# Linear attention and two MLPs on one core: k and v of a head pair loaded in two requests of 64 partitions each

## The chip, the cores and the metric

The kernel runs on one core of a Trainium2 chip. The metric is the device time of one execution in microseconds (us). TensorE (PE) multiplies matrices, VectorE (DVE), ScalarE (ACT) and GpSimd (POOL) work element by element, SyncE (SP) issues DMA requests.

## The reference

```python
kv  = einsum('bhsd,bhse->bhde', k, v)        # batch 4, heads 8, seq 576, head_dim 64
out = einsum('bhsd,bhde->bhse', q, kv)
x   = out / sqrt(mean(out*out, -1) + 1e-6) * g_norm    # then (2304, 512)
h   = x @ w_in;   x = softplus(h) @ w_out    # first MLP, 512 -> 2048 -> 512
h   = x @ w_in2;  y = leaky_relu(h, 0.01) @ w_out2     # second MLP
```

All in float32; the output is (2304, 512).

## The kernel before

The attention works in 16 units; a unit is a pair of heads of one batch entry, four units a batch entry, u even and odd alternate. 576 rows of a head don't divide into 128 partitions: 512 rows stand as 4 rows on each of 128 partitions, and 64 "left rows" remain.

`load(u)` issues the loads on SP: q, k and v of the unit, each one request [128, 2 heads, 4 rows, 64] with pieces of 1024 bytes, into rings `lda` of five buffers. At the first unit of a batch entry it also loads the left rows of all eight heads, into `ldr`: k and v as [64 partitions, 8, 64] in pieces of 256 bytes, q as two requests of 64 partitions. For b = 0 these four are issued on ACT, else on SP. The lower half of `ldr` for k and v is zeroed by POOL at the start.

`T(u)` copies q and k so that a row of two heads is contiguous (`qp`, `kp`; `copy_to`, lines 406 to 410, on ACT, DVE or POOL), transposes q on PE (line 479), forms k-transposed times v for both heads in four products (`f_kv`, line 487) and a fifth one of the left rows (`f_kvl`, line 492), masks it to two blocks (`kvm`, line 505) and copies the transposed q out of PSUM (`qt`, line 422 on DVE, 420 on ACT). At even units a transpose takes the left rows of q of this unit and the next one (line 483), copied to `qtl`. `O(u)` multiplies (line 527; left rows of two units, line 534), `normal` does the norm (`xn`), `X` transposes back (line 612, and 623 for left rows) into `xy`, by an eviction on ACT (line 600) or DVE (line 602). A float32 product appears in the trace as two records of PE, a transpose as one.

The MLPs follow: their weights are loaded and unpacked by `decode_w` (line 647 and 652 issue the loads) beside the attention; the first products of the MLP are those of line 984, six records each, among the last of the attention; most of the run is lines 894, 1151 and 1156.

The order is written by a planner at build time: each `op()` states engines and costs, and `Plan.run` places the operations on engines. Its first 500 placements are a list written out by hand, `FIRST`: a letter for the engine (E is PE, A, D, P, S, and G for requests that ACT issues) and the number of the `op()` call, counted from 0. Each engine executes its operations in that order, so one that waits holds up what stands behind it. After the list the planner chooses by its own costs.

Of the kernel before, what the change touches and what calls it, by code (L numbers as in the profile page):

```python
# [21 lines left out]
class Plan:  # L22
# [10 lines left out]
    DMA_BY = {"S": "S", "G": "A"}  # L33

    FIRST = """
    S7 E26 S0 S80 G6 S9 G5 S8 S1 G4 P40 S2 G3 D27 S85 E44 E42 S10 E32 S13 A82 S14 S15 A83 S11 A81 E29
    S24 D41 S12 D30 E45 S23 D28 D84 S38 S16 A90 E33 A31 S37 S19 E34 E46 D35 S39 D47 A36 D91 E69 A43 S17
    D87 E52 A88 S20 D48 D55 A86 E68 S18 A53 D89 P100 S22 A72 D54 A70 E102 S21 P101 E104 A92 D73 E57 D71
    S50 E60 E105 A58 S49 D103 A74 P56 D59 S51 A75 E106 D76 E61 S66 A107 D25 D78 S65 A108 E62 D79 E134
    S67 D77 A63 S110 D93 A64 E132 S109 A136 P166 E135 E116 A167 D94 P119 D95 A138 E168 D139 A117 D137  # L40
    E170 E171 A133 D118 P120 A169 E124 D96 A140 E172 E178 D97 A141 A173 E125 D142 A174 D145 A98 D144
    E126 E180 S131 E121 D127 E200 A179 D143 S129 P185 S113 A128 D186 A122 E198 D99 A123 S115 E182 A202
    P213 A199 S114 D181 E187 D203 A183 E201 S146 P212 E190 A204 E191 S111 D184 A321 S130 D205 D188 E192
    A206 S112 P236 E214 D189 E228 A207 D208 E216 P235 S175 A229 E217 S151 D211 D209 A215 A193 S176 E218
    E230 P262 D219 S177 E248 A194 D210 A231 E232 A324 S195 D220 S196 D322 E251 S197 E250 A254 A249 D325
    S222 E266 S245 A252 E264 E274 S225 D265 A233 E237 D255 D253 A147 E240 S227 E481 P263 A238 D234 S226
    A148 D149 E241 S221 A256 D150 P281 A257 S223 A275 E242 D258 S246 E267 A156 D261 S224 A243 D259 A239
    E268 A244 E276 S247 D260 A152 E283 E278 S273 D269 D277 A270 S333 D154 E297 D153 S271 E294 P308 A300
    D155 A279 S272 E286 E296 P309 S338 D282 A158 D280 S291 E287 A295 D157 D159 A298 E288 E484 S293 A284
    D299 A289 S292 A290 D160 E317 D301 E482 D161 A302 D162 A303 A318 P356 D304 E312 A285 E313 D163 P357  # L50
    D307 A164 D305 E310 E314 D306 P380 E319 A311 E353 A320 D315 P381 D165 A316 E369 A354 E368 A372 D355
    A330 E358 D373 E361 A370 E362 A359 D371 E363 E366 P396 A374 D364 A360 D365 A375 E382 A327 P397 D376
    E384 E385 A367 D379 D377 A383 E391 D378 E386 A334 E389 A392 D387 P420 E393 D328 A388 A390 E408 D336
    A394 D335 P421 D395 E409 S343 A410 E401 E402 D337 A412 A339 D413 E403 D411 A340 E398 E406 D341 A414
    D404 E485 A415 S348 A407 D416 S323 A399 D419 E429 A405 D342 A400 E431 A430 E424 D417 E422 E425 A423
    D418 A346 D345 E426 A344 E436 D432 D427 E433 D347 A428 S581 A437 S332 E439 D351 A349 E438 D350 S326
    A442 D331 A483 E450 N461 A440 E488 D352 A486 A434 D443 D441 E491 A477 D435 A451 D478 E489 A444 A445
    A463 D446 E492 A479 D449 D447 A460 E452 D490 E454 D448 E500 A453 A455 D493 D480 A487 E458 E456 D464
    N462 E503 A494 D465 A495 E504 D468 A466 D496 E501 A507 D469 E546 D467 A470 D472 E550 D510 A502 A473
    """.split()  # L60

    def __init__(self):
# [105 lines left out]
def linear_attention_two_mlps(  # L168
# [32 lines left out]
    nc = tc.nc  # L201
    B, H, S, D = q.shape
# [35 lines left out]
    def ring(pool, name, n, shape, dt=F32):  # L238
        return [pool.tile(shape, dt, name=f"{name}{i}") for i in range(n)]
# [190 lines left out]
    def load(u):  # L430
        b, hp = unit(u)
        hs = slice(2 * hp, 2 * hp + 2)
        for nm, src in (("q", q), ("k", k), ("v", v)):
            def fn(e, nm=nm, src=src):
                nc.sync.dma_start(
                    out=lda[nm][u % NLD],
                    in_=src[b, hs, 0:4 * P, :].rearrange("h (p r) d -> p h r d", r=4),
                )

            op({"S": 0.73}, fn, (), [(nm, u % NLD)])  # L440
        if u % NPAIR:
            return
        e_ = "G" if b == 0 else "S"
        for nm, src in (("k", k), ("v", v)):
            def fn(e, nm=nm, src=src):
                (nc.scalar if e == "G" else nc.sync).dma_start(
                    out=ldr[nm][b % 2][:RL], in_=src[b, :, 4 * P:S, :].rearrange("h p d -> p h d")
                )

            op({e_: 0.58}, fn, (), [(nm + "r", b % 2)])  # L450
        for x in range(2):
            def fn(e, x=x):
                (nc.scalar if e == "G" else nc.sync).dma_start(
                    out=ldr["q"][b % 2][x * RL:(x + 1) * RL],
                    in_=q[b, NPAIR * x:NPAIR * (x + 1), 4 * P:S, :].rearrange("h p d -> p h d"),
                )

            op({e_: 0.29}, fn, (), [("qr", b % 2, x)])

    def T(u):  # L460
# [29 lines left out]

        def f_kvl(e):
            nc.tensor.matmul(kv, kl[:, h2, :], vl[:, h2, :], start=False, stop=True)  # L492

        for j in range(2):
            n = 2 * P
            op(
                {"PE": 0.22 if i or j else 0.33}, lambda e, j=j: f_t(e, j),
                [("qp", i)] + ([] if i or j else [("qr", b % 2, x) for x in range(2)]), [("ps", p0 + j)],
            )
            if j:  # L500
                op({"PE": 0.88}, f_kv, [("kp", i), ("v", u % NLD)], [("ps", p1)])
                op({"PE": 0.22}, f_kvl, [("kr", b % 2), ("vr", b % 2)], [("ps", p1)])
# [11 lines left out]
            if i == j == 0:  # L514
# [883 lines left out]
```

## Time and profile before

| | us |
|---|---|
| runs shown: median (lowest to highest of 3) | 781.49 (781.37 to 782.99) |
| profiled execution, device time | 784.06 |
| span of the profiled execution | 782.1 |
| busy time of PE in it | 767.8 |

The span runs from the first to the last instruction; times of rows count from its start. A row of the timeline gives start, duration and, in brackets, the idle time before it with what ended it. Line numbers are those of the kernel before.

### The profile page before, as it was taken

How to read it: one execution, taken by the hardware profiler on the slowest of the kernel's cores; microseconds unless marked ns; L12 is line 12 of the kernel's file. 1: busy time of each engine (PE TensorE's matmuls, PEld its weight loads, DVE VectorE, ACT ScalarE, POOL GpSimd, SP SyncE). 2: the span in 40 equal slices, each digit the busy share in tenths (PEclk: the TensorE clock that was granted, in tenths of full speed). 3: DMA queues.
4: the chain of work that ended last, by engine and by line, in shares of the span. 5: the costliest groups of instructions: out<-in, count | busy, mean ns of one | idle time of the engine just before them, and what ended most of it. 6: DMA issues, size and time to landing. Idle time of an engine off the chain costs nothing.

```text
span 782.1 us, 13225 instructions
## 1 busy us (share of the span) xinstructions
PE 767.8 (98%) x5029; PEld 763.6 (98%) x5029; DVE 679.3 (87%) x1084; ACT 544.2 (70%) x930; POOL 20.9 (3%) x37
## 2 busy tenths in 40 slices
PE   6899999999999999999999999999999999999997
PEld 6899999999999999999999999999999999999997
DVE  3999999999899897996899999998899877886666
ACT  4789999788676775764588788885677645554441
POOL 2330000000000000000000000000000000000000
PEclk8999999999999999999999999999999999999999
DMA  9995768685784794683678969785875772562814
GB/s 284 289 312 166 288 225 308 248 295 200 307 321 166 266 340 150 264 304 106 255 279 293 332 213 414 306 301 193 315 268 180 279 253 104 210 246 102 299 41 122
DMA packets 80416, 192.50 MB, mean 246 GB/s; under 512 B 11616, under 2 KB 54624, under 8 KB 80352
## 3 DMA queue, kind: packets, MB, share of 16 engines
q1 hardware_dynamic: 77136, 190.47, 67.8%
q10 hardware_dynamic: 3216, 1.18, 0.6%
q8 instruction: 40, 0.66, 0.3%
q14 instruction: 24, 0.20, 0.1%
HBM read 152.31 MB, written 39.32 MB: 245 GB/s over the span
## 4 chain that ended last, share of the span: by engine, by line
PE 92%; DVE 4%; DMA 3%; issue 0%; SPq 0%; ACT 0%; DVEq 0%
PE ps L894 41%; PE ps L1151 23%; PE ps L1156 20%; PE ps L984 2%; PE ps L487 2%; PE ps L527 1%; DMA xscr<-rc 1%; DMA ka<-in_k_dram 1%; PE ps L612 1%; DMA ra<-xscr 1%; PE ps L479 1%; DVE xy L774 1%; DVE ra L740 0%; PE ps L534 0%; PE ps L492 0%
## 5 line engine op out<-in xcount | busy, mean ns | idle before, releaser
L894 PE MATMUL ps<-ra 128*128 128x384 f32 x1932 | 385.1, 335 | 0.7 <-DMA ra<-xscr 0.7
L894 PEld LDWEIGHTS ps<-ra 128*128 128x128 f32 x1932 | 332.0, 188 | 1.0 <-DMA ra<-xscr 1.0
L1151 PE MATMUL ps<-rb 128*128 128x256 f32 x1512 | 203.9, 282 | 0.0
L1156 PE MATMUL ps<-rb 128*128 128x384 f32 x1008 | 200.4, 334 | 0.0
L1151 PEld LDWEIGHTS ps<-rb 128*128 128x128 f32 x1512 | 198.0, 189 | 0.1
L923 ACT ACTIVATE rb<-mf 128x768 fp32r<-128x768 f32 x154 | 129.9, 846 | 69.5 <-PE ps L1151 39.0
L1156 PEld LDWEIGHTS ps<-rb 128*128 128x128 f32 x1008 | 177.0, 188 | 0.0
L928 DVE TENSOR_TENSOR rb<-mf,rb 128x768 fp32r<-128x768 f32 x154 | 146.7, 954 | 23.7 <-ACT rb L923 22.5
L774 DVE TENSOR_TENSOR xy<-ps,xy 128x384 f32<-128x384 f32 (+2 forms) x247 | 134.7, 549 | 32.5 <-PE ps L1151 22.0
L1008 DVE TENSOR_TENSOR mf<-mf 128x768 f32<-128x768 f32 x68 | 64.2, 953 | 2.4 <-ACT mf L909 1.8
L1201 ACT ACTIVATE mf<-ps 128x384 f32<-128x384 f32 x92 | 44.7, 489 | 30.2 <-PE ps L894 28.5
L1208 DVE TENSOR_TENSOR mf<-ps,mf 128x384 f32<-128x384 f32 x92 | 50.8, 554 | 11.6 <-PE ps L894 10.3
L1213 ACT ACTIVATE ps<-ps 128x384 f32<-128x384 f32 x46 | 22.0, 479 | 21.0 <-PE ps L894 20.9
L909 ACT ACTIVATE mf<-mf 128x768 f32<-128x768 f32 x26 | 21.9, 846 | 17.2 <-DVE mf L1208 17.0
L1073 DVE TENSOR_TENSOR rb<-rc,rb 128x512 fp32r<-128x512 f32 x44 | 29.7, 683 | 0.0
L1070 ACT ACTIVATE rb<-rc 128x512 fp32r<-128x512 f32 x44 | 27.5, 626 | 1.7 <-PE ps L1151 0.8
L915 ACT ACTIVATE mf<-mf 128x768 f32<-128x768 f32 x24 | 20.1, 839 | 9.6 <-DVE mf L1208 9.6
L1167 ACT ACTIVATE ps<-ps 128x384 f32<-128x384 f32 (+2 forms) x44 | 21.0, 479 | 7.1 <-PE ps L1156 4.3
L676 ACT ACTIVATE sqr<-mf 128x512 f16<-128x512 f32 x23 | 18.2, 790 | 7.2 <-DMA kr<-in_k_dram 6.8
L915 ACT ACTIVATE mf<-ps 128x384 f32<-128x384 f32 x32 | 15.7, 490 | 9.6 <-PE ps L894 9.4
L487 PE MATMUL ps<-va,kp 128*128 128x128 f32 x128 | 18.6, 294 | 3.5 <-DVE kp L408 3.5
L687 ACT ACTIVATE sqr<-mf 128x512 uint16<-128x512 uint16 x28 | 21.9, 783 | 0.0
(123 smaller groups left out, 747.0 us busy)
## 6 DMA issues: line engine op xcount, KB each, us to landing
ra<-xscr SPq DMA_DIRECT2D x131, 768.0 KB, 6.3
xscr<-ra SPq DMA_DIRECT2D x30, 768.0 KB, 4.9
mf<-in_moe_w_in_dram SPq DMA_DIRECT2D x18, 512.0 KB, 6.1
mf<-in_moe_w_out_dram SPq DMA_DIRECT2D x18, 512.0 KB, 6.1
lf<-in_moe_w_in_dram SPq DMA_DIRECT2D x14, 512.0 KB, 6.0
lf<-in_moe_w_out_dram SPq DMA_DIRECT2D x14, 512.0 KB, 5.1
xscr<-xy SPq DMA_DIRECT2D x8, 768.0 KB, 5.7
qa<-in_q_dram SPq DMA_DIRECT2D x16, 256.0 KB, 5.0
```

The costliest lines, as they stand in the source:

```text
L487: nc.tensor.matmul(kv, kp[i][:, r, :, :], va[:, :, r, :], start=(r == 0), stop=False)
L774: {"D": t_d(n)}, lambda e: nc.vector.tensor_tensor(dst, src, dst, ALU.add),
L894: nc.tensor.matmul(o, w_[:, a, c:c + P], e_[:, b, kk, :], start=(not on and which < 2 and kk == 0 and n == 0), stop=(kk == 1 and n == 2), ...
L915: lambda e: nc.scalar.activation(dst(), src(), AF.Prelu, alpha=0.01),
L923: {"A": t_a(n)}, lambda e: nc.scalar.activation(g[:, 0, :, :], c.ap, AF.Copy),
L928: lambda e: nc.vector.tensor_tensor(g[:, 1, :, :], c.ap, g[:, 0, :, :].bitcast(F32), ALU.subtract),
L1008: lambda e: nc.vector.tensor_tensor(to.ap, x.ap, y.ap, ALU.subtract),
L1073: lambda e: nc.vector.tensor_tensor(w_[:, 1], src(), w_[:, 0].bitcast(F32), ALU.subtract), sk + hk, lk,
L1151: nc.tensor.matmul(y[:, 256 * (j % 2):256 * (j % 2 + 1)], G_[:, a, m, js], w_[:, b, m, :], **flags)
L1156: nc.tensor.matmul(y[:, :BN], w_[:, a, m, js], G_[:, b, m, :], **flags)
L1201: {"A": t_a(BN)}, lambda e: nc.scalar.activation(c[:, m, :], src, AF.Copy),
L1208: lambda e: nc.vector.tensor_tensor(c[:, m, :], src, c[:, m, :], ALU.add),
```

## The change

k and v of a unit are each loaded in two requests over all 576 rows, nine consecutive rows to a pair of partitions: c = 0 puts five rows on partitions 0 to 63 (pieces of 1280 bytes), c = 1 four rows on partitions 64 to 127 (1024 bytes). The fifth row of partitions 64 to 127 is zeroed once for each of the ten buffers. The left rows of k and v and their products go away; `f_kv` has five products; the copy of k is 640 columns a partition, not 512. q is loaded as before; its left rows are transposed at the odd unit, not the even one, and their loads for b = 0 move from ACT to SP. The second pair of weight chunks is decoded at i = 9, not 5.

```diff
-    lda = {nm: ring(attp, nm + "a", NLD, [P, 2, 4, D]) for nm in "qkv"}
-    ldr = {nm: ring(attp, nm + "r", 2, [P, H // (2 if nm == "q" else 1), D]) for nm in "qkv"}
+    lda = {nm: ring(attp, nm + "a", NLD, [P, 2, 4 + (nm != "q"), D]) for nm in "qkv"}
+    ldr = {"q": ring(attp, "qr", 2, [P, H // 2, D])}
-    kp = ring(attp, "kp", 2, [P, 4, 2, D])
+    kp = ring(attp, "kp", 2, [P, 5, 2, D])
-    for t_ in ldr["k"] + ldr["v"]:
-        nc.gpsimd.memset(t_[RL:], 0.0)
+    for t_ in lda["k"] + lda["v"]:
+        nc.gpsimd.memset(t_[RL:, :, 4, :], 0.0)
...
+            for c in range(2):
+                def fn(e, nm=nm, src=src, c=c):
+                    nc.sync.dma_start(
+                        out=lda[nm][u % NLD][c * RL:(c + 1) * RL, :, 0:5 - c, :],
+                        in_=src[b, hs, :, :].rearrange(
+                            "h (p r) d -> p h r d", r=9
+                        )[:, :, 5 * c:5 + 4 * c, :],
+                    )
+
+                op({"S": (0.45, 0.37)[c]}, fn, (), [(nm, u % NLD, c)])
...
-            if j == 0 and i == 0:
+            if j == 0 and i == 1:
                 nc.tensor.transpose(ps[p0][:, 2 * P:3 * P], ql[:, lq, :], ident)
...
-            for r in range(4):
+            for r in range(5):
                 nc.tensor.matmul(
-                    kv, kp[i][:, r, :, :], va[:, :, r, :], start=(r == 0), stop=False
-                )
-
-        def f_kvl(e):
-            nc.tensor.matmul(kv, kl[:, h2, :], vl[:, h2, :], start=False, stop=True)
+                    kv, kp[i][:, r, :, :], va[:, :, r, :], start=(r == 0), stop=(r == 4)
+                )
...
-        if i in (3, 5):
+        if i in (3, 9):
```

`FIRST` is new, with 517 entries; its first lines:

```diff
+    E32 S7 S10 S0 S9 S6 S8 P46 S11 S88 E51 S5 A33 S1 S2 A47 S4 E52 S3 S16 S13 A91 E35 E48 S12 A53 E37
+    S14 A89 D54 S17 D34 A49 S21 A36 E38 S15 S20 S18 E76 D39 D50 S19 A40 D90 P64 S93 E77 D92 A78 E60 S42
+    A80 P108 D63 S41 D81 E65 A61 D79 S27 E110 E67 D62 S30 E113 E68 S29 D109 A82 S22 A83 A111 D84 S23
+    E114 A69 S28 D85 A70 A96 S43 D66 E140 D112 S24 A98 D115 E124 D86 S44 A116 A154 S45 D87 E142 D99 A94
+    S26 D31 D95 S25 A125 D127 E159 E143 S55 A144 E129 D126 E156 S57 P155 A146 A141 E131 D145 S71 P128
```

Counting the `op()` calls gives the names. SP's requests (c0 and c1 are the halves of k or v, ql the left rows of q, w a chunk of weights): before, in the order q1, q0, w, v1, k1, k0, v0, w, q2, q3, k3, v3, k2, ..., k15 last. After: q1, v1c0, q0, k1c1, ql, k1c0, v1c1, w, ql, k0c0, k0c1, v0c1, v0c0, v2c1, k2c0, q2, k2c1, q3, v3c1, v2c0, v3c0, k3c0, k3c1, w, k5c0, q5, ql, g_norm twice, q4, k4c0, ql, k5c1, k4c1, v5c0, v5c1, v4c1, v4c0, q6, k6c1, q7, k7c0, v7c1, k6c0, q8, v6c1, v6c0, k7c1, k8c0, v7c0, k8c1, v8c1, k10c0, v8c0, ..., v15c1 last. PE (T transposes of q, kv its products, numbers are units): after, T1, kv1, T0, T1, T0, kv0, O1, left rows, O0, T2, T3, T2, T3, kv2, kv3, X0, O2, O3, T5, left rows, T4, T5, T4, X1, kv5, kv4, ..., T6, O4, T6, X3, T7, kv6, T8, T7, kv7, T8, kv8; before, unit 8's products stand behind O6, O7, T9, X4, X5 and a first product of line 984, which after stand behind them. Over the whole list the engines of the copies of k are: before 4 DVE, 1 ACT, 11 POOL; after 2, 1, 13. Of q: before 2 DVE, 14 POOL; after 2 DVE, 2 ACT, 12 POOL. Of the masks: 10 DVE and 6 ACT, then 8 and 8; of qt: 7 DVE and 25 ACT, then 4 and 28; of qtl: 2 DVE and 6 ACT, then 5 and 3; of the left rows' evictions: 3 DVE and 4 ACT, then 7 ACT.

## Rows read from the trace of the kernel before

**Rows 1.** The page: busy us, share of the span and instructions.

```profile
PE 767.8 (98%) x5029; PEld 763.6 (98%) x5029; DVE 679.3 (87%) x1084; ACT 544.2 (70%) x930; POOL 20.9 (3%) x37
```

**Rows 2.** Stretches: PE, PEld, DVE, ACT, POOL busy (x instructions), granted clock, DMA share, GB/s.

```profile
15.00:25.00 10.00, 8.09 (x71) 7.83 (x70) 9.67 (x22) 7.33 (x20) 3.91 (x6) 1.00 1.05 316
...
40.00:45.00 5.00, 5.00 (x43) 4.88 (x41) 4.59 (x13) 4.93 (x15) 1.24 (x2) 1.00 1.09 363
...
45.00:50.00 5.00, 5.00 (x44) 4.97 (x43) 4.90 (x11) 4.08 (x11) 1.43 (x2) 1.00 0.95 245
...
80.00:120.00 40.00, 40.00 (x232) 39.71 (x231) 39.95 (x54) 36.98 (x64) 0.00 (x0) 1.00 0.73 277
```

**Rows 3.** PE's waits up to 82 us: waited for, us in total, times, longest.

```profile
PE ps L487 <- DVE kp L408: 3.5, 1, 3.5
...
PE ps L527 <- DVE xn L590: 1.7, 1, 1.7
...
PE ps L483 <- DMA qr<-in_q_dram: 1.6, 1, 1.6
```

**Rows 4.** Timeline of PE: start, duration, line, operation, records merged.

```profile
10.91 3.78 PE L487 MATMUL ps<-va,kp 128*128 128x128 f32 x16 [3.46 <-DVE kp L408]
...
14.48 0.65 PE L492 MATMUL ps<-vr,kr 128*128 128x128 f32 x4
...
18.67 1.06 PE L487 MATMUL ps<-va,kp 128*128 128x128 f32 x8
...
42.35 1.05 PE L487 MATMUL ps<-va,kp 128*128 128x128 f32 x8
...
43.24 0.39 PE L492 MATMUL ps<-vr,kr 128*128 128x128 f32 x2
...
67.07 1.06 PE L487 MATMUL ps<-va,kp 128*128 128x128 f32 x8
...
71.33 4.44 PE L984 MATMUL ps<-ra 128*128 128x384 f32 x24
```

**Rows 5.** A stretch of 1 us, columns as in rows 2.

```profile
12.00:13.00 1.00, 1.00 (x7) 1.00 (x7) 0.30 (x1) 0.58 (x2) 0.00 (x0) 0.50 1.06 372
```

**Rows 6.** Issues by line on SP: count, duration ns min/median/max, first and last start.

```profile
L435 SPq DMA_DIRECT2D ka<-in_k_dram x16: 367/472/933, 3.0 to 52.9; - x16
...
L446 SPq DMA_DIRECT2D kr<-in_k_dram x3: 607/612/657, 16.2 to 46.9; - x3
...
L453 SPq DMA_DIRECT2D qr<-in_q_dram x6: 596/615/1347, 19.4 to 43.4; - x6
...
L1246 SPq DMA_DIRECT2D graw<-in_g_norm_dram x2: 495/542/590, 12.5 to 13.8; - x2
```

**Rows 7.** Timeline of SP's issues, and POOL's first copy.

```profile
0.73 0.96 SPq L435 DMA_DIRECT2D qa<-in_q_dram  x2
...
3.76 0.62 POOL L410 TENSOR_SCALAR qp<-qa 128x512 f32<-128x512 f32 x1
...
10.33 0.47 SPq L435 DMA_DIRECT2D ka<-in_k_dram  x1
...
10.84 0.47 SPq L435 DMA_DIRECT2D va<-in_v_dram  x1
...
52.93 0.93 SPq L435 DMA_DIRECT2D ka<-in_k_dram  x1
```

**Rows 8.** Groups by line and shape to 82 us; count, busy us, mean ns, idle before.

```profile
L408 DVE COPY kp<-ka 128x512 f32<-128x512 f32 x4 | 1.7, 422 | 5.7 <-DMA ka<-in_k_dram 5.6
...
L406 ACT ACTIVATE kp<-ka 128x512 f32<-128x512 f32 x1 | 0.6, 624 | 0.0
...
L410 POOL TENSOR_SCALAR kp<-ka 128x512 f32<-128x512 f32 x11 | 8.4, 760 | 7.0 <-DMA ka<-in_k_dram 3.4 <-PE ps L487 2.0 <-PE ps L612 0.8
...
L381 POOL MEMSET kr<- 64x512 f32 x2 | 1.0, 523 | 0.1
...
L422 DVE COPY qt<-ps 128x256 f32<-128x256 f32 x7 | 2.9, 413 | 0.2 <-PE ps L479 0.2
```

More of the change, by code (lines that the diff above doesn't have):

```diff
@@ L41 @@
[L41 to L45, printed above, removed]
@@ new lines @@
+    A161 S58 D152 E170 S73 A162 E188 A133 S118 D101 E190 A171 S74 A134 A189 S119 P176 D102 E191 E179
+    S121 D103 A194 E172 A333 P202 S164 D104 S120 A192 E177 D105 E218 S136 P225 A173 D334 E204 S165 A219
+    E180 P203 S137 D174 A178 S135 A336 D193 E227 S138 P226 E207 E208 A205 D195 S123 D181 A196 D182 A197
+    S139 D206 A106 D198 E229 S163 E230 S122 D201 A209 D199 S167 E220 D200 P294 A231 E222 S166 A221 D210
+    S252 D337 P273 E240 S257 A223 S185 P272 D224 E238 S183 A242 P293 E241 S184 E277 D243 A244 E278 A239
@@ new lines @@
+    S187 D245 S186 D107 A246 S211 E286 A247 A232 E274 S212 A228 E297 D248 A287 S213 E295 E298 D279 S215
+    A275 D251 D250 A280 S235 A254 D249 S214 E288 E308 A253 S281 D255 P320 A289 S233 D299 A276 D256 E290
+    A258 P321 S236 A310 S285 D260 E306 A291 S217 D259 E309 E489 D311 A296 P368 S234 A300 A312 D292 S237
+    A307 P369 E325 S216 D313 E322 D261 A314 E326 S283 A315 A323 D316 S345 A262 A324 S302 E329 A264 D319
+    D317 S282 E331 E370 P390 S284 A332 D327 E365 D318 A328 S350 A339 D265 S303 E372 E378 A330 S301 P406
@@ L60 @@
+    A445 D432 A361 D362 E446 D363 A442 D491 E458 A440 A448 D443 E447 N469 E496 A494 D449 A450 A459 D451
+    E497 D364 A452 A453 A471 D454 E499 A485 D457 D455 A487 E460 A498 E462 D488 E500 A463 D456 A461 D486
+    A468 E464 D472 E466 N470 E508 S594 D473 S335 A501 D476 A474 E511 A495 D475 E512 D477 A515 D480 A478
+    E509 D518 A513 A502 E529 D479 S675 A510 D522 S341 A503 E526 D516 A519 E527 A542 D504
     """.split()
@@ L433, in load @@
         for nm, src in (("q", q), ("k", k), ("v", v)):
[L434 to L437, printed above, removed]
-                )
-            op({"S": 0.73}, fn, (), [(nm, u % NLD)])
+            if nm == "q":
+                op(
+                    {"S": 0.73}, lambda e: nc.sync.dma_start(
+                        out=lda["q"][u % NLD],
+                        in_=q[b, hs, 0:4 * P, :].rearrange("h (p r) d -> p h r d", r=4),
+                    ), (), [("q", u % NLD)],
+                )
+                continue
+            for c in range(2):
[7 more added lines that the diff above has]
+                op({"S": (0.45, 0.37)[c]}, fn, (), [(nm, u % NLD, c)])
         if u % NPAIR:
             return
[L443 to L447, printed above, removed]
-                )
-            op({e_: 0.58}, fn, (), [(nm + "r", b % 2)])
         for x in range(2):
             def fn(e, x=x):
-                (nc.scalar if e == "G" else nc.sync).dma_start(
+                nc.sync.dma_start(
                     out=ldr["q"][b % 2][x * RL:(x + 1) * RL],
@@ L463, in T @@
         i = u % 2
-        for nm, dst in (("q", qp), ("k", kp)):
+        engines = "AD" if u == 0 else "ADP"
+        for nm, dst, n in (("q", qp, 4), ("k", kp, 5)):
             copy_to(
-                dst[i], lda[nm][u % NLD].rearrange("p h r d -> p r h d"), 512,
-                [(nm, u % NLD)], [(nm + "p", i)], "AD" if u == 0 else "ADP",
+                dst[i], lda[nm][u % NLD].rearrange("p h r d -> p r h d"), n * P,
+                [(nm, u % NLD)] if nm == "q" else [(nm, u % NLD, c) for c in range(2)],
+                [(nm + "p", i)], engines,
             )
@@ L471, in T @@
         kv = ps[p1][:, 2 * P:3 * P]
-        ql, kl, vl = (ldr[nm][b % 2] for nm in "qkv")
+        ql = ldr["q"][b % 2]
         lq = slice(2 * (hp % 2), 2 * (hp % 2) + 2)
@@ L496, in T @@
             op(
-                {"PE": 0.22 if i or j else 0.33}, lambda e, j=j: f_t(e, j),
-                [("qp", i)] + ([] if i or j else [("qr", b % 2, x) for x in range(2)]), [("ps", p0 + j)],
+                {"PE": 0.33 if i and not j else 0.22}, lambda e, j=j: f_t(e, j),
+                [("qp", i)] + ([("qr", b % 2, x) for x in range(2)] if i and not j else []), [("ps", p0 + j)],
             )
             if j:
-                op({"PE": 0.88}, f_kv, [("kp", i), ("v", u % NLD)], [("ps", p1)])
-                op({"PE": 0.22}, f_kvl, [("kr", b % 2), ("vr", b % 2)], [("ps", p1)])
+                op(
+                    {"PE": 1.1}, f_kv, [("kp", i)] + [("v", u % NLD, c) for c in range(2)],
+                    [("ps", p1)],
+                )
                 def f_m(e):
@@ L513, in T @@
             from_psum(qt[i][:, j * n:(j + 1) * n], ps[p0 + j][:, :n], n, p0 + j, [("qt", i, j)])
-            if i == j == 0:
+            if i and not j:
                 ql_ = qtl[u // 2 % 2].rearrange("p (a n) -> p a n", n=RL)[:, ::2, :]
@@ L1286, in linear_attention_two_mlps @@
        + [("qt", i, j) for i in range(2) for j in range(2)]
-       + [(t, i) for t in "qkv" for i in range(NLD)]
-       + [(t + "r", i) for t in "kv" for i in range(2)]
+       + [("q", i) for i in range(NLD)]
+       + [(t, i, c) for t in "kv" for i in range(NLD) for c in range(2)]
        + [("qr", i, x) for i in range(2) for x in range(2)])
```

31 lines of the change are left out of this document (9 added, 22 removed).

## Prediction

> **What bounds the kernel now.** I read the page first, then the busy time by stretch, the waits of TensorE (PE), its timeline and the issue costs of SyncE (SP). The page says PE: busy for 98% of the span [rows 1]. So only idle PE time can be won. By stretches PE has 8.09 busy of 10 us at 15 to 25, and all of 40 to 50 and of 80 to 120 [rows 2]. The waits before 82 us that are over 1 us are three that work ends: 3.5 us before the first k-v product (for the copy of k), 1.7 before an O product (for xn), 1.6 before the left rows of q [rows 3]. [...] From 42.35 eight records take 0.89, so 0.111 each at full clock [rows 4]; the slow ones lose 16 x 0.112 = 1.8 us. Together: 8.6 us, the 1.7 at 15 to 25 and the rest before. That is what a better start can win.
>
> Behind PE stand two more near-limits: DMA with 363 GB/s at 40 to 45 and a busy share of 1.09, and VectorE (DVE) with 39.95 busy of 40 us from 80 to 120 [rows 2].
>
> **The products.** Four products and one of left rows per head pair become five: 10 records either way, 16 x 10 x 0.111. PE's work is unchanged, and so is everything after the attention. The result is the lead that PE wins at the start, less what is given back.
>
> **SP's queue.** This decides, as it is the only queue of loads. Removed are 8 loads of k, v left rows, 2 of them with ACT; 32 loads of 128 partitions become 64 of 64. The issues on SP up to the last k, v load grow from 16 + 32 + 12 to 16 + 64 + 8 (the b = 0 loads of q's left rows come over from ACT), plus six weight loads and graw's two. A load on 128 partitions takes SP 0.37 at least and 0.47 in the median; those on 64 partitions take 0.61 with 512 pieces, 0.615 with 256, 0.54 with 64 [rows 6]. The new ones have 128 pieces on 64 partitions, a shape that the trace doesn't have. Bounds: 0.37 and 0.65. I take 0.57, between the two nearest rows (0.54 and 0.61). Between issues lie 0.04 (10.33 + 0.47 to 10.84) [rows 7]. So 0.61 for a half load, 0.49 for a load of q and, taken alike, of weights, 0.65 for q's left rows, 0.58 for graw: 64 x 0.61 + 22 x 0.49 + 8 x 0.65 + 2 x 0.58 = 56 us. The last is issued near 56 us, against 52.93 now [rows 7]. SP was idle at times; now it never is, and it paces the loads. A load lands 3.0 us after its issue when nothing is ahead (q1 issued at 0.73, its copy starts at 3.76) [rows 7].
>
> Now the new order, waypoint by waypoint.
> - First product (unit 1). Ahead of k1's second half stand q1, a half, q0, a half, one load of q's left rows: 0.73 + 0.49 + 0.61 + 0.49 + 0.61 + 0.65 = 3.6, lands at 6.6. The weight load that stood third is now behind. The last half of v1 is issued at 4.2 and lands at 7.2. The copy of k is 640 columns on ACT, 0.62 x 1.25 = 0.78 [rows 8]: 7.4. The product starts at 7.4 instead of 10.91: 3.5 us earlier. I expect the half clock here too, since PE has nothing from the first transposes, by about 5, to 7.4; the 1.8 us stay lost.
> - Unit 3. Before the second half of k3 stand 4 q, 1 weight load, 2 left rows, 15 halves: 0.73 + 1.96 + 0.49 + 1.3 + 9.15 = 13.6. It lands at 16.6, is copied on DVE in 0.42 x 1.25 = 0.53 [rows 8], product at 17.2 instead of 18.67 [rows 4]. About 1 us of PE idle goes here.
> - Units 5 and 4: the last half of v4 is issued at 22.4 and lands at 25.4; PE could be there at 24.6. 0.8 idle.
> - Unit 8: the last half of v8 is issued 9.4 later, at 31.8, and lands at 34.8, when PE has waited 1.1 us. The product ends at 35.9. Before, it ended at 43.4 [rows 4], but with 33 more records and the first six of the MLP ahead of it: 33 x 0.111 + 1.0 = 4.7, so 38.7 for the same work. The lead is 2.7 us.
> - From there each load lands by the time that PE comes for it (v11 at 46 against about 47; the last of v15 at 60 against 65), and I let the lead stand until the run of plain products that starts at 71.33 [rows 4] and through the MLP.
>
> **Small parts.** Copies of k: 25% longer; on GpSimd (POOL) 13 x 0.95 for 11 x 0.76 [rows 8], hidden, since POOL has over half of its time free [rows 2]; without that cover it would be 4 us on DVE. DVE has 2 k copies instead of 4 and 4 qt copies instead of 7: 2 x 0.53 - 4 x 0.42 - 3 x 0.41 = -1.9 us [rows 8]; three left-row copies come and three evictions go, of one size; two masks go to ACT, so DVE is relieved by about 2.5. ACT gets these, about 3.5 us, and loses idle time that it has. Ten memsets of 64 x 128 for four of 64 x 512: the four take 0.52 each [rows 8]; ten at a quarter to the whole of that are 1.3 to 5.2, and I take 2, no change: they end by about 3.8, when q1 is there. At 5.2 the first copy comes 3 us late and the first product waits 0.2 more.
> The left rows of q move to the odd unit: nothing waits, as their transpose stands behind the first k-v product, by when (7.4 + 10 slow records = 9.6) the second part, issued at 5.3, has landed at 8.3.
> Left rows were moved in 256-byte pieces. At 45 to 50, where the last of these move (issued up to 46.9) [rows 2, 6], the rate was 245 GB/s with a busy share of 0.95, against 363. Larger pieces can win up to 1 or 2 us of transfer time, but transfers no longer pace.
>
> **The sum.** Against the profiled run (784.06, span 782.1): 784.1 - 2.7. The runs of before have their median at 781.49, 2.6 below the profiled one; what lies around the span and the profiling are in both, so I take the difference to the median: 781.5 - 2.7 = 778.8.
>
> **Rivals.**
> 1. Loads on 64 partitions move slower. The halves and q's left rows are 9.96 MB, q and weights 7.34 MB. The second at 363 GB/s [rows 2] are 20.2 us. With a start at 2 and 1 for the landing, the last product of k and v (67.07 now, 4.3 before 71.33 [rows 4]) may come at 66.7 without loss, since what follows it is 0.4 longer. So the halves need (66.7 - 3 - 20.2) = 43.5 us, 229 GB/s. At 245, the rate of the stretch with most 64-partition loads, nothing is lost; at half of 363 the product comes at 78, 11 us late. In the middle, 213 GB/s: 46.8 + 20.2 + 3 = 70.0, 3.3 late: 784.8, slower. For it: each half touches half of the partitions. Against: the 64-partition loads of before stood in stretches of 245 to 316 GB/s [rows 2], but with few bytes in them. [...]
> 2. The lead is given back. DVE is busy for 39.95 of 40 us from 80 to 120 [rows 2]; if PE reaches it 2.7 us earlier than DVE's backlog allows, PE waits there: 781.5, no change. Against: DVE has 2.5 us less to do and starts earlier.
> 3. An issue of a half load costs 0.37, as on 128 partitions: 36 halves stand before unit 8's last, 7.2 us, and the loads no longer pace. Of the 8.6 us remain the first wait, then 2.1, and the slow clock, 1.8: a gain of 4.7, 776.8; if the clock doesn't fall in the shorter pause, 775.0. At the dear end, 0.65, 36 x 0.08 = 2.9 are lost and the gain is gone: 781.7.
>
> **How the numbers follow.** Forecast 0.47 (777 to 780), rival 1 0.20, rival 2 0.13, rival 3 at its cheap end 0.11 and at its dear end 0.09. A measurement of this kernel can tell 0.2%, 1.6 us, from no change. Faster: 0.45 + 0.11 = 0.56; within: 0.02 + 0.13 + 0.07 = 0.22; slower: 0.20 + 0.02 = 0.22. The range takes in rival 3's cheap end and goes into rival 1: 775.0 to 784.0.
>
> **What would show it.** Right: half loads at 0.57 on SP back to back from 0.7 to 56; the first k-v product at 7.4; unit 8's near 35; the first of the run of plain products at 68.6; same records of PE. Rival 1: halves that land 5 us or more after their issue while the GB/s are below 230. Rival 2: PE idle for DVE between 75 and 120. Wrong altogether: PE waits before 25 us as long as before, or another wait of over 1 us after 40.

## The result and the profile after

The kernel after takes 792.1 us (median of 4 runs, 791.5 to 793.4); the kernel before, run beside it on the same chip, 781.75. The ratio is 1.0134, 95% interval [1.0121, 1.0147]: 10.4 us slower, where 2.7 us faster were predicted, and 8 us above the top of the range. The profiled execution took 792.64 with a span of 790.8.

The page of the kernel after, busy time by engine, and its chain that ended last:

```profile
PE 772.8 (98%) x5029; PEld 766.5 (97%) x5029; DVE 678.3 (86%) x1078; ACT 545.3 (69%) x938; POOL 20.9 (3%) x43
...
PE 92%; DMA 4%; ACT 2%; SPq 1%; issue 1%; DVE 0%; POOL 0%; POOLq 0%; DVEq 0%; ACTq 0%
```

PE has the same 5029 records as in [rows 1]; no work was added, yet its busy time is 5.0 us longer. By stretches (columns as in [rows 2]), first the kernel after, then a row of before:

```profile
5.00:20.00 15.00, 10.04 (x45) 8.98 (x44) 3.65 (x8) 4.86 (x11) 1.45 (x2) 1.00 0.88 228
15.00:25.00 10.00, 9.95 (x64) 9.57 (x63) 6.50 (x16) 4.36 (x12) 1.45 (x2) 1.00 1.01 241
20.00:70.00 50.00, 42.66 (x344) 39.53 (x344) 40.64 (x92) 37.63 (x97) 13.39 (x19) 1.00 0.93 240
40.00:45.00 5.00, 3.98 (x34) 3.61 (x34) 4.35 (x11) 1.87 (x6) 1.06 (x3) 1.00 1.00 249
45.00:50.00 5.00, 4.15 (x37) 3.94 (x36) 3.53 (x8) 3.45 (x10) 2.42 (x4) 1.00 0.71 166
...
80.00:120.00 40.00, 39.76 (x236) 38.60 (x235) 39.13 (x60) 38.31 (x70) 0.00 (x0) 1.00 0.65 244
```

```profile
20.00:70.00 50.00, 47.75 (x399) 45.67 (x398) 46.59 (x110) 41.74 (x105) 15.32 (x21) 1.00 0.87 263
```

Where before has no idle PE at all [rows 2], 40 to 50 us, after has 1.9 us of it. From 20 to 70 us PE loses 5.1 us of busy time and 55 records against before. From 80 on both are dense, so the loss is made by then. PE's waits up to 82 us (against [rows 3]) and its timeline (against [rows 4]) show for what:

```profile
PE ps L493 <- DMA va<-in_v_dram: 3.8, 5, 1.0
PE ps L493 <- ACT kp L407: 2.9, 1, 2.9
PE ps L485 <- POOL qp L411: 2.4, 2, 1.5
PE ps L489 <- DMA qr<-in_q_dram: 1.8, 2, 0.9
PE ps L493 <- DVE kp L409: 1.2, 1, 1.2
```

```profile
8.12 2.50 PE L493 MATMUL ps<-va,kp 128*128 128x128 f32 x10 [2.86 <-ACT kp L407]
...
14.48 2.50 PE L493 MATMUL ps<-va,kp 128*128 128x128 f32 x10 [1.23 <-DVE kp L409]
...
21.74 2.70 PE L493 MATMUL ps<-va,kp 128*128 128x128 f32 x20
...
43.17 1.35 PE L493 MATMUL ps<-va,kp 128*128 128x128 f32 x10 [1.02 <-DMA va<-in_v_dram]
...
82.00 3.22 PE L990 MATMUL ps<-ra 128*128 128x384 f32 x17
```

The first product does come earlier: 8.12 for 10.91. But from then on PE waits again and again for a load that has only just landed or for the copy behind it, up to unit 15, and the run of plain products starts at 82.00, not 71.33: 10.7 us late. (The two spans differ by 8.7 us only: behind that start PE is idle for 5.7 us in this trace of before, whose time is 2.6 above the median, and for 3.6 in that of after.) Up to that start, before and after:

```profile
0.00:71.33 71.33, 62.73 (x495) 59.94 (x495) 55.74 (x133) 51.07 (x123) 20.94 (x37) 0.95 0.88 266
0.00:82.00 82.00, 67.63 (x495) 62.80 (x495) 55.30 (x128) 54.31 (x132) 20.89 (x43) 1.00 0.90 238
```

The same 495 records stand before it. PE is idle for 14.4 us instead of 8.6, and busy with them for 67.6 instead of 62.7: of the 10.7 us, 5.8 are waits and 4.9 are slower records. Ten records of the product at 14.48 take 2.50 us, twenty of that at 21.74 take 2.70. Where PE is fed, a record starts every 0.213 us up to 20.45 us and every 0.11 behind it. That is half pace for 45 records, 4.6 us by these two steps, for 16 records and 1.6 us in before. The column of the granted clock says 1.00 there because the trace has no clock record before 20.45; in before the same pace stands beside 0.50 [rows 5].

SP's issues (as in [rows 6]) and parts of its timeline (as in [rows 7]):

```profile
L445 SPq DMA_DIRECT2D ka<-in_k_dram x32: 595/598/1297, 2.6 to 68.3; - x32
L445 SPq DMA_DIRECT2D va<-in_v_dram x32: 595/602/1434, 1.2 to 70.3; - x32
```

```profile
5.26 0.59 SPq L653 DMA_DIRECT2D mf<-in_moe_w_in_dram  x1
...
9.80 0.60 SPq L445 DMA_DIRECT2D ka<-in_k_dram  x1
12.10 0.37 SPq L437 DMA_DIRECT2D qa<-in_q_dram  x1
...
15.73 1.25 SPq L445 DMA_DIRECT2D ka<-in_k_dram  x2
...
25.71 3.37 SPq L445 DMA_DIRECT2D va<-in_v_dram  x4
...
39.18 0.60 SPq L445 DMA_DIRECT2D va<-in_v_dram  x1
...
69.67 1.24 SPq L445 DMA_DIRECT2D va<-in_v_dram  x2
```

A half load costs 0.595 at least and 0.60 in the median, none less, where a load on 128 partitions costs 0.37 and 0.47 [rows 6]. The last load is issued at 70.3 instead of 52.93 [rows 7]. The gap from 10.40 to 12.10 is a second limit: SP stands idle until the weight load of 5.26 lands, at 12.08. That was the load issued eight before. In the traces of before and after no load on SP starts earlier than 0.016 us after the load issued eight before it has landed, and here gaps of 5.0 us end within 0.12 us of such a landing. The operands of the issues in the trace say why: a load tells of its landing by a semaphore (a counter), the loads on SP use eight of them in turn, and of the 95 issues up to 90 us that use one again, 94 wait for it. So this limit is written into the program.

### The profile page after: what moved, and what is told of

Read it like the earlier page. It is cut to its first block, busy times and chain, and to the rows that moved or that the text cites. A ratio compares the mean times of both kernels' runs of the same rounds, so it can differ in the third digit from the quotient of the medians.

```text
span 790.8 us, 13283 instructions
## 1 busy us (share of the span) xinstructions
PE 772.8 (98%) x5029; PEld 766.5 (97%) x5029; DVE 678.3 (86%) x1078; ACT 545.3 (69%) x938; POOL 20.9 (3%) x43
## 4 chain that ended last, share of the span: by engine, by line
PE 92%; DMA 4%; ACT 2%; SPq 1%; issue 1%; DVE 0%; POOL 0%; POOLq 0%; DVEq 0%; ACTq 0%
PE ps L900 42%; PE ps L1157 23%; PE ps L1162 22%; DMA mf<-in_moe_w_in_dram 2%; PE ps L990 1%; PE ps L493 1%; PE ps L533 1%; DMA mf<-in_moe_w_out_dram 1%; SPq L445 1%; DMA qr<-in_q_dram 1%; DMA ka<-in_k_dram 1%; DMA va<-in_v_dram 0%; ACT xy L606 0%; PE ps L485 0%; PE ps L540 0%
## 5 line engine op out<-in xcount | busy, mean ns | idle before, releaser
L493 PE MATMUL ps<-va,kp 128*128 128x128 f32 x160 | 23.6, 300 | 8.1 <-DMA va<-in_v_dram 3.8
L493 PEld LDWEIGHTS ps<-va,kp 128*128 128x128 f32 x160 | 21.1, 209 | 10.5 <-ACT kp L407 3.3
L693 ACT ACTIVATE sqr<-mf 128x512 uint16<-128x512 uint16 x30 | 23.5, 784 | 4.8 <-DMA mf<-in_moe_w_in_dram 4.0
```

What stands on the lines that cost most here:

```text
L493: nc.tensor.matmul(kv, kp[i][:, r, :, :], va[:, :, r, :], start=(r == 0), stop=(r == 4))
```

## The theories and the runs

**S**: SP paces the loads up to unit 15, by the price and the number of its requests. **P**: transfers that reach half of the partitions move slower (rival 1 of the prediction). **L**: the new order list or the fifth product loses the time. All times below are medians, with the range of the runs; ratios are against the kernel before, run beside them.

**1 and 2. The kernel before, its k and v loads cut in two** requests, in halves of the partitions or in even and odd ones:

```diff
-                nc.sync.dma_start(
-                    out=lda[nm][u % NLD],
-                    in_=src[b, hs, 0:4 * P, :].rearrange("h (p r) d -> p h r d", r=4),
-                )
+                # run 2: slice(0, P, 2), slice(1, P, 2)
+                for x in [slice(None)] if nm == "q" else [slice(0, RL), slice(RL, P)]:
+                    nc.sync.dma_start(
+                        out=lda[nm][u % NLD][x],
+                        in_=src[b, hs, 0:4 * P, :].rearrange(
+                            "h (p r) d -> p h r d", r=4
+                        )[x],
+                    )
```

> The kernel before, in which each load of k and v of 512 rows is issued as two requests, partitions 0 to 63 and 64 to 127; nothing else changes. Theory S (SP's issue paces: a request on 64 partitions takes SP 0.60 us and 0.05 to 0.1 until the next, whatever it moves): 32 loads cost 2 x 0.65 instead of 0.5 each, 26 us more of SP by 53 us, of which about 17 were idle: the last load some 9 us later, 787 to 792. Theory P (requests that touch only one half of the partitions are moved slowly by the DMA engines): slower too, 786 to 792, with packets of 1024 bytes well above their 46 ns and busy engines at 230 to 250 GB/s. Theory L (the new order list is what costs): no change, 781 to 783.

> As the kernel before, but each load of k and v is two requests of 64 partitions, the even and the odd ones. Same number of requests, pieces and bytes as with halves. Theory S: as slow as the version with halves, 787 to 792, since SP issues the same. Theory P: the engines reach both halves, so about the time of before, 782 to 784. Theory L: 781 to 783.

Measured: 794.4 (793.2 to 795.6), 1.0152 [1.0136, 1.0168], and 792.4 (791.5 to 793.9), 1.0129 [1.0110, 1.0147]. The issues of k, halves first:

```profile
L436 SPq DMA_DIRECT2D ka<-in_k_dram x32: 595/604/1855, 4.6 to 72.1; - x32
```

```profile
L436 SPq DMA_DIRECT2D ka<-in_k_dram x32: 601/605/1487, 5.1 to 71.2; - x32
```

With the old order list and the old products the loss is as large, so L falls. Even and odd partitions lose nearly as much as halves: the price of an issue is the same 0.60, and P can be 2.0 us of 12 here (the ranges of the two runs overlap). Both came out above what S expected; that the 12 loads of left rows on SP, which this kernel keeps, are the reason is likely but not shown.

**3. The kernel after, with five rows on the even partitions and four on the odd ones** (the fifth row is zeroed on all partitions).

```diff
-                        out=lda[nm][u % NLD][c * RL:(c + 1) * RL, :, 0:5 - c, :],
+                        out=lda[nm][u % NLD][c:P:2, :, 0:5 - c, :],
```

> The changed kernel with the five rows on the even partitions and the four rows on the odd ones, instead of 0 to 63 and 64 to 127; the fifth row of all partitions is zeroed at the start. Theory S: as the changed kernel, 791 to 793. Theory P: the 10 us come back, 779 to 783. Theory L: 791 to 793.

Measured: 789.8 (789.5 to 790.7), 1.0095 [1.0079, 1.0111]. Below what S expected, and far above what P did. Halves cost 2.3 us more than even and odd partitions, in runs that don't overlap (3.0 by the two ratios, as the runs of before beside them differ by 0.8); 7.4 of the 10.4 us remain by the ratio. From 20 to 70 us:

```profile
20.00:70.00 50.00, 43.66 (x352) 40.14 (x351) 41.63 (x93) 39.97 (x102) 14.67 (x20) 1.00 0.84 254
```

More bytes move than in after (254 for 240 GB/s) with a smaller DMA share (0.84 for 0.93): P is real, and the small part.

**4. One request per tensor**, 128 partitions with 1152 bytes a head (four and a half rows, so that the products pair other rows), all else as in after but the memsets:

```diff
-        nc.gpsimd.memset(t_[RL:, :, 4, :], 0.0)
+        nc.gpsimd.memset(t_[:, :, 4, D // 2:], 0.0)
...
-                        out=lda[nm][u % NLD][c * RL:(c + 1) * RL, :, 0:5 - c, :],
...
+                    if c == 0:
+                        nc.sync.dma_start(
+                            out=lda[nm][u % NLD].rearrange("p h r d -> p h (r d)")[:, :, 0:288],
+                            in_=src[b, hs, :, :].rearrange("h s d -> h (s d)").rearrange(
+                                "h (p n) -> p h n", n=288
+                            ),
+                        )
```

> The changed kernel, its order and its work on the engines, but k and v of a unit come in one request of 128 partitions with the same bytes (pieces of 1152 bytes, 4.5 rows a partition), at the place of the first half; the second half issues nothing. The rows land in other places, so the output is not the reference's. Theory S and theory P: both limits are gone, 777 to 782. Theory L: above 786.

Measured: 780.3 (780.0 to 783.7), 0.9977 [0.9966, 0.9989]. Its issues of k and its stretch:

```profile
L446 SPq DMA_DIRECT2D ka<-in_k_dram x16: 367/467/775, 3.0 to 44.7; - x16
```

```profile
20.00:70.00 50.00, 49.24 (x409) 46.73 (x407) 48.36 (x109) 46.24 (x116) 17.38 (x22) 1.00 0.83 275
```

Same bytes, same order list, same five products: with half as many requests for k and v the loss is gone and 1.8 us are won by the ratio. L is out for good, and S stands; P would have gone with it, so this run doesn't part the two.

**5. Few bytes, all requests**: in after, from the sixth unit on each half load brings only its first row, and the products use what the buffers hold.

```diff
+                    n = 5 - c if u < NLD else 1
-                        out=lda[nm][u % NLD][c * RL:(c + 1) * RL, :, 0:5 - c, :],
+                        out=lda[nm][u % NLD][c * RL:(c + 1) * RL, :, 0:n, :],
...
-                        )[:, :, 5 * c:5 + 4 * c, :],
+                        )[:, :, 5 * c:5 * c + n, :],
```

> The changed kernel, but from the sixth unit on each half load of k and v carries only its first row (pieces of 256 bytes, a fourth or a fifth of the bytes); the output is not the reference's, as the rest of a buffer keeps older rows. Requests, partitions and order are the same. Theory S (SP's issue of 0.60 us for each request on 64 partitions paces the loads): nearly the time of the version with even and odd partitions, 787 to 791, because SP still issues 64 of them; the half loads still take 0.60. If the bytes pace (theory P, or the DMA engines at all): 779 to 783.

Measured: 788.2 (787.0 to 788.9), 1.0082 [1.0063, 1.0101].

```profile
L446 SPq DMA_DIRECT2D ka<-in_k_dram x32: 595/604/623, 2.7 to 62.6; - x32
```

```profile
20.00:70.00 50.00, 44.53 (x364) 41.71 (x363) 42.97 (x96) 40.86 (x105) 18.62 (x22) 1.00 0.57 165
```

The DMA engines are busy for 0.57 of the time, and yet PE has 3.2 us less of busy time here than in before (after: 5.1 less). An issue with pieces of 256 bytes costs the same, 0.595 at least and 0.60 in the median: the bytes don't set it. SP waits for 0.5 us only, so this is the price alone: 6.6 of the 10.4 us.

**6 and 7. The second halves of v issued elsewhere**, by POOL or by ACT:

```diff
-                    nc.sync.dma_start(
+                    (nc.gpsimd if e == "H" else nc.sync).dma_start(   # run 7: nc.scalar, "G"
...
-                op({"S": (0.45, 0.37)[c]}, fn, (), [(nm, u % NLD, c)])
+                op({"H" if c and nm == "v" else "S": (0.45, 0.37)[c]}, fn, (), [(nm, u % NLD, c)])
```

> The changed kernel with the second half of each load of v issued by GpSimd instead of SP, at the same place of the order. Theory S: SP has 16 issues of 0.69 us with their gaps less, 11 us, and its last load goes out near 59 instead of 70: 783 to 787. Theory P: same transfers, so 790 to 793.

> As the version with GpSimd, but ScalarE issues the second halves of v. Theory S: SP gains the same 11 us, but ScalarE loses 16 x 0.65 = 10 us of the first 80, where it is busy for some 55 of 65: between 784 and 790. Theory P: 790 to 795.

Measured: 790.0 (789.4 to 791.8), 1.0112 [1.0088, 1.0136], and 794.7 (793.2 to 795.5), 1.0164 [1.0144, 1.0184]. Both miss what S expected and lie where P did, so what follows is read from their traces. With POOL, its issues and SP's of k; then the largest of POOL's waits, and with ACT the largest of SP's:

```profile
L445 SPq DMA_DIRECT2D ka<-in_k_dram x32: 595/597/1332, 2.7 to 63.3; - x32
L445 POOL DMA_DIRECT2D va<-in_v_dram x16: 587/646/767, 4.0 to 64.0; - x16
...
POOL kp L411 <- DMA ka<-in_k_dram: 19.3, 6, 9.7
```

```profile
SPq L445 <- DMA va<-in_v_dram: 9.3, 6, 3.8
```

With POOL, SP is relieved of 16 issues and yet ends at 64.6: its own waits grow to 11.4 us, and of 12.8 us in gaps over 0.1 us, 11.9 end as the load eight before has landed; POOL stands for 19.3 us before copies of k, and what it issues stands behind them. With ACT, all 15 gaps over 0.2 us on SP up to 64 us end within 0.09 us after the load that used the same semaphore before has landed, and for 7 of them (the 6 of the row, 9.3 us, and one before a load of q) that is a half of v that ACT had issued: ACT's loads draw on the same eight semaphores as SP's (POOL's have eight others), so that a late issue on ACT holds up SP. S as price alone is not enough.

**8. The kernel before with twice the requests, all on 128 partitions** (rows 0 and 1, rows 2 and 3):

```diff
+                for x in [slice(None)] if nm == "q" else [slice(0, 2), slice(2, 4)]:
+                    nc.sync.dma_start(
+                        out=lda[nm][u % NLD][:, :, x, :],
...
```

> The kernel before, in which each load of k and v is two requests on all 128 partitions, rows 0 to 1 and rows 2 to 3 (pieces of 512 bytes). As many requests as with halves of the partitions. Theory S: a request on 128 partitions takes SP 0.37 to 0.45, so 32 x (2 x 0.43 - 0.53) = 11 us more, and SP waited about 12 us in all: 782 to 786, far below the 794.4 and 792.4 of the versions with 64 partitions. If the number of requests as such costs: 790 or more.

Measured: 787.5 (785.6 to 790.7), 1.0078 [1.0049, 1.0108], between what S expected (up to 786) and what the number as such was to cost (790 or more).

```profile
L436 SPq DMA_DIRECT2D ka<-in_k_dram x32: 368/464/994, 3.7 to 65.5; - x32
```

At the cheap price 100 requests still end at 65.5. Over half of the loss (5.8 of 10.4 us) needs no partition half and no price of 0.60. Pieces of 512 bytes are another difference here, so run 11 asks the same with large ones.

**9. 116 partitions with five rows, in one request**: 115 x 5 + 1 = 576 rows.

```diff
+    NP5 = 116
...
+                        n = NP5 - (u == NU - 1)
+                        nc.sync.dma_start(
+                            out=t_[:n].rearrange("p h r d -> p h (r d)"),
+                            in_=bass.AP(
+                                tensor=at.tensor, offset=at.offset,
+                                ap=[[5 * D, n], [S * D, 2], [1, 5 * D]],
+                            ),
+                        )
...
-                    kv, kp[i][:, r, :, :], va[:, :, r, :], start=(r == 0), stop=(r == 4)
+                    kv, kp[i][:NP5 - (r > 0), r, :, :], va[:NP5 - (r > 0), :, r, :],
+                    start=(r == 0), stop=(r == 4)
```

> The kernel after, with k and v of a head pair in one request of 116 partitions with 5 rows a head (the last partition's rows 1 to 4 are left out of the products, which take 115 partitions there; the last unit has a second request of one partition). No half loads and no memsets; the same five products and the same order list. Theory S (SP's 64 issues at 0.60 and what waits behind them pace the loads): an issue falls back to 0.37 to 0.5, the last load of k and v is issued at 44 to 48 us instead of 70, and the time is 779.5 to 782.0. Rival P (what is lost comes from partitions that carry uneven bytes, the rest of the 12 partitions idle): above 784. Rival L (order list or the fifth product): above 786.

Measured: 840.9 (840.3 to 841.8), 1.0745 [1.0730, 1.0760]: none of the theories. The stretch from 22 to 26 us:

```profile
22.00:26.00 4.00, 4.00 (x21) 4.00 (x20) 3.52 (x7) 1.26 (x3) 1.61 (x2) 0.50 0.27 98
```

The DMA share is 0.27 with 98 GB/s, as if about a quarter of the engines carried such a request; why is not shown. From 20 to 70 us it is 0.38 with 126 GB/s, against 0.93 and 240 with 64 partitions (after) and 0.83 and 275 with 128 (run 4). With transfers as slow as these the run says nothing on S; in after, with a DMA share of 0.93, this is not the cause.

**10. The kernel before with the first weight load behind the loads of the first two units**, alone:

```diff
-    S7 E26 S0 S80 G6 S9 G5 S8 S1 G4 P40 S2 G3 D27 S85 ...
+    S7 E26 S0 G6 S9 G5 S8 S1 S80 G4 P40 S2 G3 D27 S85 ...
```

> The kernel before with one change to its order list: the first weight load, third on SP's queue, goes behind the loads of k and v of the first two units. If the kernel of one request per tensor wins its 1.5 to 2 us by an earlier first k-v product alone, this one wins them too: 779.5 to 781.0, the first k-v product at 7.5 to 9.5 instead of 10.91. If the weights are then late for the first products of the MLP, or the lead is given back before 80 us: 781.5 to 783.

Measured: 781.7 (780.8 to 783.0) beside 782.4, 0.9991 [0.9982, 0.9999]. The first product starts at 8.62, then PE waits 2.1 us for v, and the run of plain products starts at 70.43, 0.9 earlier. So the move alone wins 0.7 us, at the edge of what can be told from nothing, where run 4 won 1.8. It is below what was expected if an earlier first product were all (779.5 to 781.0).

**11. The same 64 requests, cut as 112 partitions with five rows and 16 with one:**

```diff
+    NP5 = 112
...
+                    if c == 0:
+                        nc.sync.dma_start(
+                            out=t_[:NP5],
+                            in_=src[b, hs, 0:5 * NP5, :].rearrange("h (p r) d -> p h r d", r=5),
+                        )
+                    else:
+                        nc.sync.dma_start(
+                            out=t_[NP5:, :, 0, :],
+                            in_=src[b, hs, 5 * NP5:S, :].rearrange("h p d -> p h d"),
+                        )
...
```

> The kernel after with the same 64 requests for k and v, the same bytes and the same five products, but the rows of a head are cut otherwise: 112 partitions with 5 rows in the first request, 16 partitions with one row in the second. (The number 116 moved the loads at 98 GB/s and a DMA share of 0.22 for long stretches, as if few engines took part; 112 and 16 are multiples of 16.) Theory S (price of an issue times their number): the request of 112 partitions costs 0.37 to 0.5, the one of 16 partitions 0.3 to 0.6 (bounds from the cheapest issue and from the 0.60 of 64 partitions); with 0.45 for both and the small gaps of after the last load is issued at 48 to 60 and the time is 780 to 785. Rival (the number of requests, since SP waits for the request eight issues earlier to land, sets the loss): last load at 64 or later as with two 128-partition requests per tensor, 786 to 789.

Measured: 787.75 (786.6 to 788.2), 1.0066 [1.0045, 1.0087]: the rival's number, not S's. Issues of k (the 16 partitions first), its stretch, and some of SP's waits:

```profile
L453 SPq DMA_DIRECT2D ka<-in_k_dram x16: 311/445/605, 2.2 to 62.9; - x16
L448 SPq DMA_DIRECT2D ka<-in_k_dram x16: 312/426/602, 3.5 to 61.4; - x16
```

```profile
20.00:70.00 50.00, 43.74 (x350) 41.48 (x350) 41.71 (x91) 39.29 (x99) 15.97 (x22) 0.97 0.90 251
```

```profile
SPq L453 <- DMA mf<-in_moe_w_in_dram: 3.3, 1, 3.3
SPq L453 <- DMA ka<-in_k_dram: 1.6, 4, 0.5
...
SPq L448 <- DMA qa<-in_q_dram: 1.1, 3, 0.4
```

The price has fallen to 0.43 to 0.45, and the last load is still issued at 64.4, as SP now waits 14 us. A load of k waits for a transfer of weights or of q, with which it shares no buffer. Of 14.5 us in gaps over 0.1 us, 13.6 end within 0.12 us after the landing of the request issued eight before. Eight small requests in flight are fewer bytes in flight than eight large ones; that this is why SP comes to wait is argued, not shown. The 0.97 is a later stretch at a granted clock of 0.50, from 55.1 to 58.5 us, which costs PE up to 1.7 us in this execution.

**12. One request per tensor, 128 partitions with five rows each**, so that the last 12 read on into the next head and the products leave them out:

```diff
+                    n = P if u < NU - 1 else NP5   # the last unit: 112 and 16 as in run 11
...
+                                ap=[[5 * D, n], [S * D, 2], [1, 5 * D]],
...
+                n = (P if u == NU - 1 else 116) if r == 0 else (NP5 if u == NU - 1 else 115)
                 nc.tensor.matmul(
...
+                    kv, kp[i][:n, r, :, :], va[:n, :, r, :], start=(r == 0), stop=(r == 4)
```

> The kernel after with one request per tensor and head pair: 128 partitions with 5 rows each from row 5p on, so that the last 12 read 64 rows of the next head, which the products leave out (they take 116 partitions for the first row, 115 for the others); 11% more bytes of k and v. The last unit has two requests, 112 partitions with 5 rows and 16 with one. No memsets. Theory S: last load issued at 46 to 52, time 780 to 782.5 (the kernel with one request of 1152-byte pieces took 780.28; 1.0 MB more at 275 GB/s is 3.8 us of transfers, which do not pace). Rival (transfer rate paces from there): 783 to 785.

Measured: 781.1 (780.6 to 783.5), 0.9992 [0.9980, 1.0005]: S's number. With 11% more bytes of k and v the loads move at 293 GB/s from 20 to 70 us:

```profile
20.00:70.00 50.00, 49.21 (x409) 46.71 (x409) 48.25 (x110) 46.21 (x116) 17.32 (x22) 1.00 0.88 293
```

No kernel that computes the whole of the reference beat the kernel before by more than the 0.1% of run 10.

## What the runs say together

SP's account up to its last load of k or v, worked out from all issue rows of SP in each trace (waits are gaps over 0.2 us; "run" is the start of the run of plain products; times in us):

| kernel | requests | issuing | small gaps | waits | last issue | run starts | time |
|---|---|---|---|---|---|---|---|
| one request, 1152 bytes (4) | 64 | 31.6 | 3.3 | 11.7 | 46.9 | 69.6 | 780.3 |
| one request, five rows (12) | 66 | 31.7 | 3.2 | 15.0 | 50.4 | 69.9 | 781.1 |
| weights later (10) | 68 | 36.2 | 3.8 | 11.6 | 51.7 | 70.4 | 781.7 |
| before | 68 | 37.7 | 3.7 | 11.7 | 52.9 | 71.3 | 781.75 |
| 112 and 16 partitions (11) | 96 | 45.7 | 4.8 | 14.0 | 64.4 | 77.9 | 787.75 |
| before, rows in two (8) | 100 | 51.2 | 5.8 | 8.2 | 65.6 | 76.1 | 787.5 |
| few bytes (5) | 96 | 58.1 | 5.9 | 0.5 | 64.6 | 76.6 | 788.2 |
| after, even and odd (3) | 96 | 58.2 | 6.2 | 2.2 | 66.7 | 78.3 | 789.8 |
| second halves of v on POOL (6) | 80 | 48.5 | 4.6 | 11.4 | 64.6 | 79.0 | 790.0 |
| after | 96 | 59.1 | 5.7 | 5.4 | 70.3 | 82.0 | 792.1 |
| before, even and odd (2) | 100 | 61.7 | 5.8 | 3.5 | 71.2 | 81.6 | 792.4 |
| before, halves (1) | 100 | 61.6 | 5.9 | 4.4 | 72.1 | 83.8 | 794.4 |
| second halves of v on ACT (7) | 80 | 49.9 | 4.3 | 17.4 | 71.8 | 83.9 | 794.7 |

(The times stand beside runs of before between 781.6 and 782.5; in runs 6 and 7 SP's requests alone are counted.) The time follows the last issue: from 46.9 to 52.9 it moves by 1.5 us, and from 64.4 to 72.1 by 6.6 (787.8 to 794.4). Two limits lie close together at 96 requests. One is the price: 0.60 on 64 partitions, with a small gap each. The other is the eight requests in flight: taking away the price (run 11) brings the second out, and taking away the bytes, and with them the waits (run 5), leaves the first. Of what was tried, only fewer requests remove both. From after, even and odd partitions give 2.3 us, the cheaper issue 2.1 more (789.8 to 787.75), one request instead of two another 6.7 (to 781.1); by the ratios these are 3.0, 2.3 and 5.8, and in another sequence of steps the parts would be other ones.

## Why the prediction was wrong, point by point

**SP's sum** is the step that failed, in size and in what it was carried to. Forecast were 52.3 us of issues and 3.8 of gaps, last issue near 56; measured are 59.1, 5.7 of small gaps and 5.4 of waits, last issue at 70.3.
- The half load: 0.57 was put between two rows of 64 partitions by the number of their pieces [rows 6]. Its mean is 0.63: 64 x 0.06 = 3.9 us. For q, k and v the price went by partitions, not by pieces: 0.595 at least with 128 pieces of 1280 bytes and with pieces of 256 bytes alike (run 5). The dear bound, 0.65, was the near one; the row at 0.54 (graw, two issues on 64 partitions, 0.495 and 0.59) was the misleading one. In the kernel after these took 0.60.
- Loads of q and weights: 0.53 and 0.55 for 0.45; left rows 0.72 for 0.61 (the 0.65 held a gap of 0.04); together 2.7 us.
- Small gaps: 0.07 for 0.04, 1.9 us. Waits: 5.4 us for nothing. "SP was idle at times; now it never is" took SP's idle time in the trace of before for free time. A part of it was the wait for a landing: there too gaps of 4.9 us end as the request eight before has landed.
- The landing: 3.0 us behind an issue "when nothing is ahead" was taken for every load. Something was ahead:

```profile
DMA to landing us min/median/max: 2.7/4.3/6.6
```

(loads of v in after).

**"From there each load lands by the time that PE comes for it, and I let the lead stand"** is where the sign was lost. The lag of the loads against the forecast grows with each request: 2.8 us at k3's second half (issued 16.38 for 13.6), 7.4 at v8's (39.18 for 31.8), 14 at the last. The forecast followed SP to unit 8 and then compared v15's landing, 60, with PE's 65. It landed at 76.7, of which 6.4 us were the way from issue to landing. A queue that paces has to be summed to its last request; the dear end of rival 3 was carried by 36 x 0.08 to unit 8 only, and so came out at no change. Of the signs that were given for "wrong altogether", one came: a wait of 1.02 us at 43.17.

**"The 1.8 us stay lost"** was a term mis-sized. The slow records behind it are the 16 from 10.91 to 14.48, 0.223 us each for 0.111 from 42.35 on [rows 4], beside a granted clock of 0.50 [rows 5]. The half pace was taken to end with the first product; the left rows of q and the loads of unit 0 came late too, PE stood idle again before 12.35 and 14.48, and by its pace the slow clock lasted up to 20.45: about 4.6 us instead of 1.8. Late loads are so paid twice, in waits and in slow records behind them; that the second follows from the first is read from the order in this trace, and no run took it apart.

**Rival 1** (64 partitions move slower) has the right sign and at its far end, half of 363 GB/s, the right size, but its mechanism is the smaller part: 2.0 us (run 1 against 2) and 2.3 to 3.0 us (run 3). That the far end fits is luck: its own sign, landings of 5 us or more below 230 GB/s, didn't come (4.3 in the median, 240 GB/s). Run 4, with one request of 128 partitions in place of two to disjoint halves, takes 11.8 us less than after; by runs 3 and 5 the pace of the transfers is the smaller part of that, too.

**What held.** PE's records are the same in number. The first product came at 8.12 for a forecast of 7.4 (10.91 before). Removing the left rows and the weight load from the front wins, but 1.8 us (run 4), not 2.7. Copies, masks and memsets cost nothing that can be seen: in run 4 all of them but the memsets' size are as in after. Rival 2 (DVE) didn't come up, as there was no lead to give back: from 80 to 120 it is busy for 39.13 us of 40 [rows 2: 39.95].

**What stays open.** What more than eight semaphores would win: the eight are the program's, and no run had more. Whether the chip has a limit of its own behind them doesn't show. Why one request wins 1.8 us in run 4 where the weight load alone wins 0.7 in run 10: the rest may be the left rows in small pieces or their requests, which no run took apart.

## What to carry to other kernels

Before splitting a load, sum its queue to the last request and compare that with when the consumer needs it, at the dearest row of the same partition count. Count requests, not bytes: here some 30 more on one queue were 10 us at the dear price and 6 at the cheap one. If idle time of an issuing engine ends as an earlier transfer lands, it isn't free (5.0 us of such gaps in after, 13.6 in run 11): look which semaphore it waits for, and which load had it before. And here a load was better kept on 128 partitions in one request (run 4, 780.3 us for 792.1), also with rows read past the end to save the second one (run 12, 781.1).

## What had not been expected of the hardware

- The price of an issue of k or v goes by partitions: 0.60 us on 64, whether halves or every second one, and at least 0.31 on 112 or 16 and 0.36 on 128. Why 64 is the dearest is not shown. Cheap issues get dearer among dear ones: the loads of q, on 128 partitions, took 0.55 in the median in after and 0.43 in run 4.
- Requests of 116 partitions moved at 98 GB/s with a DMA share of 0.27, and cost 58 us in all (run 9).
- Loads issued by SP and by ACT share eight semaphores in this program, and a load waits until the one that used its semaphore before has landed (94 of 95 on SP in after). A late load on one engine so holds up the other (run 7: six waits of SP, 9.3 us, for halves of v that ACT had issued).
- A granted clock of 1.00 in the column can mean that no clock record was there: in the trace of after the records begin at 20.45 us (4.33 in before), and up to there PE runs at half pace. The pace of like records, 0.213 against 0.11 us, tells the two levels apart.
